# A two-phase FFN behind attention and a mixture of experts: buffers, conversions and token loads of its first phase rearranged

## Chip, cores and metric

One core of one Trainium2 chip. The time is device microseconds of a whole execution; that of a kernel is the median of its runs.

## What is computed

Linear attention over 4 x 8 heads, 576 positions and 64 features, then a routed mixture of 8 experts over the 2304 tokens, then a dense feed-forward network, all in float32 accuracy. The change lies in the last of the three:

```python
def _moe2_ref(x, w_in, w_out):            # x 2304 x 512, w_in 512 x 2048, w_out 2048 x 512
    h = x @ w_in
    g = np.maximum(0.01 * h, h)
    return (g @ w_out).astype(np.float32)

def reference(**kwargs):
    ...
    attn_out = _attn_ref(**attn_kwargs)
    ...
    x = _moe_ref(x=x, **moe_kwargs)
    return _moe2_ref(x=x, **moe2_kwargs)
```

The weights of the FFN arrive as float64, seen by the kernel as 64-bit integers.

## The kernel before

Every product is taken in three matmuls: both operands are split into a high and a low part (fp32r), and high x high, high x low and low x high are added in PSUM. `parts` (L1411, L1412) makes such a pair: ScalarE copies the value rounded to the high part, VectorE subtracts it to get the low part.

Attention and the experts come first (up to about 464 us of the profiled span); the experts leave their result, transposed, in DRAM as `yt`. The class `Ffn` does the rest. Its tokens are 9 groups j of 256, its hidden features 8 blocks b of 256. All work is in the order in which the program issues it: each engine takes its own instructions in that order, and waits in place where an operand or a buffer isn't ready. SP's queue, which issues the DMAs, is in order too.

**Phase one** makes h = leaky(x @ w_in). A step `first(b, j)` is 24 matmuls of 256 columns into one PSUM bank (four banks take turns). Then `leaky` (L1431, L1432): ScalarE writes 0.01 x bank into a tile `t`, VectorE takes the maximum of `t` and the bank, and `keep` (L1435) has SP store `t` in DRAM (`gd`, 256 KB). The bank is free after VectorE, the tile after the store has landed. The pool of `t` has 3 buffers. Block 0 and block 1 come interleaved, over all groups; blocks 2 to 7 follow, 9 steps each: 68 steps in `run`, the 4 other of the 72 products being made while the experts end (two by `wide`, whose halves `narrow` finishes at the start of `run`).

The tokens of the groups 4 to 8 are loaded in `run`: `load` (L1395) asks SP for 512 KB of `yt`, `x_split` makes the two parts.

The weights: `fetch` (L1345) asks SP for one block of float64, 1 MB, into the tile `wraw`. `cv1` (L1353 to L1356) takes the absolute value and the low words on ScalarE, sign and limits on VectorE; `cv2` joins exponent and mantissa on VectorE (L1361) and adds the rounding bits on GpSimd in two halves (L1363). Then for w_in (block numbers 0 to 7) `cv3` splits the result `af` into two parts; for w_out (8 to 15) `sums` (L1379 to L1381) makes 7 sums and differences of quarters of the block and `cv4` splits these. `wraw` has one buffer (tag raw) and `af` one. Weights 0 and 1 are converted long before; the other 14 here, two within each 9 steps. A table `work` in `run` says after which step each of these calls is issued.

**Phase two** makes h @ w_out in 7 products of halves instead of 8. `back` (L1455) loads two blocks of one group (512 KB) into one of three buffers of the pool f_raw, `combine` (L1462 to L1464) makes the sums on VectorE, `ready(k)` calls for a further combine where k is even, and splits one block's seven operands into the pair g[k] (five buffers in turn). `second(k)` is 21 matmuls (L1494). After 8 of them the group's result lies in four banks; `post` adds it up in four parts, multiplies by the token's gate, and `scatter` (L1534) has GpSimd write the rows by an indirect DMA. Four g are prepared ahead.

Of the kernel before, what the change touches and what calls it, by code (L numbers as in the profile page):

```python
# [8 lines left out]
F32 = mybir.dt.float32  # L9
# [4 lines left out]
I64 = mybir.dt.int64  # L14
AF = mybir.ActivationFunctionType
# [42 lines left out]
NB = 8  # L58
NG = 9
HELD = 4  # L60
PRODUCTS = ((1, 0), (5, 5), (0, 4), (4, 3), (2, 6), (6, 1), (3, 2))
CONVERT = 8

# [1224 lines left out]
class Ffn:  # L1288
# [23 lines left out]
    def open_x(self, ctx):  # L1312
        self.pad(ctx, "f_pad1", 48)
        self.slots.update(dict.fromkeys(("x0", "xh", "xl", "x3"), self.pool(ctx, "f_x0", 1)))
        self.t_p = self.pool(ctx, "f_t", 3)
        h, l = [self.slot(t, 2048, t).rearrange("p (j k n) -> p j k n", j=2, n=256) for t in ("xh", "xl")]
        self.wide_x = h, l
        for j in range(HELD):
            self.xs[j] = (h[:, j - 1], l[:, j - 1]) if j in (1, 2) else self.x_slot(j)
# [5 lines left out]
    def open_rest(self, ctx):  # L1325
        p = lambda n, b: self.pool(ctx, n, b, side="right")
        q = lambda n, b: self.pool(ctx, n, b, space=PSUM)
        self.pad(ctx, "f_pad2", eng=self.nc.gpsimd, side="right")
        self.slots.update(dict.fromkeys([f"{m}{b}" for m in "hl" for b in range(NB - 3)], p("f_v", 1)))
        self.slots.update(dict.fromkeys([f"x{j}" for j in range(HELD, NG)], p("f_x1", 1)))  # L1330
        self.raw_p, self.cv_p = p("f_raw", 3), p("f_cv", 1)
        self.early = False
        self.apart = p("f_apart", 1).tile([128, 8], F32, name="f_apart")
        ps_o = q("ps_o", 4)
        self.ps_o = lambda: ps_o.tile([128, DM], F32, tag="po", name="po")

        def ps_l():
            pool, tag = self.banks[self.turn % 4]
            self.turn += 1
            return pool.tile([128, 512], F32, tag=tag, name="pl")  # L1340
        self.turn, self.ps_l = 0, ps_l

    def fetch(self, i):
        t = self.cv_p.tile([128, 1024], I64, tag=("w0", "w2")[i] if self.early else "raw", name="wraw")
        self.nc.sync.dma_start(out=t, in_=self.wd[i])  # L1345
        half = lambda dt, j: t.bitcast(dt).rearrange("p (n t) -> p n t", t=2)[:, :, j]
        self.d[i] = {"hi": half(I32, 1), "hf": half(F32, 1), "lo": half(U32, 0), "li": half(I32, 0)}

    def cv1(self, i):
        nc, d = self.nc, self.d[i]  # L1350
        t = d["af"] = self.cv_p.tile([128, 2048], F32, tag=("w1", "w3")[i] if self.early else "af", name="af")
        d["f"], d["a"] = t[:, 0:1024].bitcast(I32), t[:, 1024:]
        nc.scalar.activation(d["a"], d["hf"], AF.Abs, scale=2.0 ** 16)  # L1353
        nc.scalar.activation(d["li"], d["lo"], AF.Copy, scale=2.0 ** -29)
        nc.vector.tensor_scalar(d["f"], d["hi"], -0x80000000, None, ALU.bitwise_and)
        nc.vector.tensor_scalar(d["a"], d["a"], F64_MAX, F64_MIN, ALU.min, ALU.max)  # L1356
# [94 lines left out]
    def back(self, p):  # L1451
        if p < NG * NB // 2:
            j, q = divmod(p, NB // 2)
            t = self.raws[p] = self.raw_p.tile([128, 1792], F32, tag="raw", name="raw").rearrange("p (b s n) -> p b s n", b=2, n=128)
            self.nc.sync.dma_start(out=t[:, :, 0:4], in_=self.gd[j][q].rearrange("p (b s n) -> p b s n", b=2, n=128))  # L1455

    def combine(self, p):
# [8 lines left out]
    def ready(self, k):  # L1466
        if k >= NG * NB:
            return
        p = k // 2
        if k % 2 == 0:  # L1470
            self.combine(p + 1)
        tag = ("wb", "x6", "x7", "wa", "x8")[k % 5]
        o = 0 if tag[0] == "w" else 16
# [24 lines left out]
    def post(self, j, part, last=False):  # L1498
# [11 lines left out]
        if part == 1:  # L1510
# [1 line left out]
            V.tensor_tensor(u[:, 1:3], u[:, 3:4].to_broadcast([128, 2, 256]), p1.rearrange("p (m n) -> p m n", n=256), ALU.add)  # L1512
            V.tensor_tensor(c0[:, h0], u[:, 1], p1[:, h1], ALU.add)
            if last:
                nc.scalar.activation(u[:, 0], u[:, 0], AF.Copy, scale=g1)
        elif part == 2:
            V.tensor_tensor(c0[:, h1], u[:, 1], p2[:, h0], ALU.add)
            nc.scalar.activation(c0, c0, AF.Copy, scale=g0)
            self.scatter(2 * j, c0)
            V.tensor_tensor(c1[:, h0], u[:, 2], p2[:, h1], ALU.add)  # L1520
            if last:
                nc.scalar.activation(c1[:, h0], c1[:, h0], AF.Copy, scale=g1)
        else:
            if last:
                V.scalar_tensor_tensor(c1[:, h1], p3[:, h0], g1, u[:, 0], ALU.mult, ALU.add)
            else:
                V.tensor_tensor(c1[:, h1], u[:, 0], p3[:, h0], ALU.add)
                nc.scalar.activation(c1, c1, AF.Copy, scale=g1)
            self.scatter(2 * j + 1, c1)
            del self.ms[j]  # L1530

# [9 lines left out]
    def run(self, ctx):  # L1541

        self.open_rest(ctx)
        self.load(HELD)
        self.load(HELD + 1)
        self.fetch(2)
        for j in range(HELD + 2, NG):
            self.load(j)
        self.narrow()
        steps = [(1, 1), (1, 2)] + [(b, j) for j in range(3, NG) for b in range(2)]  # L1550
        work = {5: [(self.cv1, 2)], 6: [(self.cv2, 2), (self.fetch, NB)], 7: [(self.cv3, 2)],
                10: [(self.cv1, NB)], 11: [(self.cv2, NB), (self.fetch, 3)], 12: [(self.sums, NB)], 13: [(self.cv4, NB)]}
        for s in (2, 4, 6, 8, 10):
            work.setdefault(s, []).insert(0, (self.x_split, HELD + s // 2 - 1))
        for b in range(2, NB):
            at = len(steps)
            steps += [(b, j) for j in range(NG)]
            i, o = b + 1, NB + b - 1
            if b < NB - 1:
                todo = {0: [(self.cv1, i)], 1: [(self.cv2, i), (self.fetch, o)], 2: [(self.cv3, i)], 4: [(self.cv1, o)],  # L1560
                        5: [(self.cv2, o), (self.fetch, i + 1 if b < NB - 2 else o + 1)], 6: [(self.sums, o)]}
                if b < NB - 2:
                    todo[7] = [(self.cv4, o)]
            else:
                todo = {0: [(self.back, 0), (self.back, 1)], 2: [(self.cv4, o - 1)], 3: [(self.cv1, o), (self.back, 2)],
                        4: [(self.cv2, o), (self.fetch, o + 1)], 5: [(self.sums, o), (self.cv4, o)],
                        6: [(self.combine, 0), (self.ready, 0)],
                        7: [(self.cv1, o + 1), (self.ready, 1)], 8: [(self.cv2, o + 1), (self.ready, 2), (self.ready, 3)]}
            for n, w in todo.items():
                work[at + n] = w  # L1570
        for s, (b, j) in enumerate(steps):
            self.first(b, j)
            for f, i in work.get(s, ()):
                f(i)
        end = NG * NB
        for k in range(end - 4):
            self.second(k)
            if k < 2:
                (self.sums, self.cv4)[k](2 * NB - 1)
# [233 lines left out]
```

## Time and profile before

| | us |
|---|---|
| Median of 3 runs (874.27 to 882.2) | 874.45 |
| The profiled execution | 873.44 |
| Its span in the profile | 871.2 |
| TensorE busy with matmuls (96% of the span) | 833.3 |
| VectorE busy (66%) | 574.1 |
| ScalarE busy (51%) | 440.5 |
| GpSimd busy (20%) | 172.6 |

The profile is one execution on the chip; times in it count from the start of its span. PE is TensorE (PEld its weight loads), DVE VectorE, ACT ScalarE, POOL GpSimd, SPq the queue of SP. In a row of a timeline stand start, duration, engine, line, operation, output and inputs, the number of like instructions merged into it, and in brackets the idle time of the engine ahead of it and what ended it. A merged row of several instructions of a queue spans from the first one's start to the last one's end. "pl" and "po" are PSUM banks, "t" the tile of an activation, "y" a loaded token group, "wraw" and "af" the two stages of a converted weight, "raw<-gd" a back.

### The profile page before, as it was taken

What the parts mean: (1) busy time and instruction counts of PE and PEld (TensorE: products, weight loads), DVE (VectorE), ACT (ScalarE), POOL (GpSimd) and SP (SyncE); (2) the same over time, 40 slices, a digit from 0 to 9 for tenths busy, and PEclk for the clock granted to TensorE, in tenths of its full rate; (3) what the DMA queues carried; (4) which work ended last, traced back from release to release, by engine and by line L of the source; (5) the groups of instructions that cost most, each with busy time, mean ns of one, the idle gap of its engine ahead of it and who ended that gap; (6) DMA issues with size and microseconds to landing.
All of it is one profiled execution on the core that took longest, in us unless ns stands there. A gap on an engine that the chain in (4) does not pass through costs nothing.

```text
span 871.2 us, 17587 instructions
## 1 busy us (share of the span) xinstructions
PE 833.3 (96%) x6850; PEld 819.3 (94%) x6850; DVE 574.1 (66%) x1065; ACT 440.5 (51%) x837; POOL 172.6 (20%) x236
## 2 busy tenths in 40 slices
PE   9999999999999999999998899999999599999996
PEld 8999999999999999999997789988999499999996
DVE  7678666876964275556771455555555898888883
ACT  7777666666343345466761444444343443445442
POOL 5345223322120110014300112121210201111112
PEclk9999999999999999999999899999999799999998
DMA  6452332162175234657747244535446334444431
GB/s 201 135 158 87 110 102 88 57 203 77 55 289 190 67 124 154 229 166 247 242 130 239 80 153 151 193 126 190 151 166 217 121 121 130 138 134 158 145 122 49
DMA packets 60809, 128.32 MB, mean 147 GB/s; under 512 B 5448, under 2 KB 24520, under 8 KB 58672
## 3 DMA queue, kind: packets, MB, share of 16 engines
q1 hardware_dynamic: 57520, 117.30, 41.0%
q0 software_dynamic: 3056, 9.70, 3.1%
q8 instruction: 56, 0.92, 0.4%
q14 instruction: 33, 0.27, 0.1%
q10 hardware_dynamic: 144, 0.13, 0.1%
HBM read 93.81 MB, written 33.29 MB: 146 GB/s over the span
## 4 chain that ended last, share of the span: by engine, by line
PE 68%; DVE 7%; DMA 7%; issue 5%; POOL 5%; ACT 5%; SPq 1%; POOLq 0%; ACTq 0%; DVEq 0%
PE po L1494 10%; PE pl L1494 9%; PE py L1208 8%; PE pp L1167 8%; PE kv L195 7%; PE nm L259 7%; PE pj L165 5%; DMA gd<-t 5%; POOL af L1363 4%; PE pl L1419 2%; DVE af L1361 2%; DMA wraw<-in_wd_dram 2%; PE dt L201 2%; PE py L1176 1%; PE ye L1027 1%
## 5 line engine op out<-in xcount | busy, mean ns | idle before, releaser
L1419 PE MATMUL pl<-x,wi 128*128 128x256 f32 x1296 | 157.6, 282 | 14.9 <-ACT x L1411 7.3
L1419 PEld LDWEIGHTS pl<-x,wi 128*128 128x128 f32 x1296 | 153.3, 192 | 18.9 <-DVE t L1432 8.1
L1494 PE MATMUL po<-wo,g 128*128 128x256 f32 x840 | 100.6, 282 | 10.6 <-ACT g L1411 8.0
L1494 PEld LDWEIGHTS po<-wo,g 128*128 128x128 f32 x840 | 99.1, 192 | 11.8 <-ACT g L1411 8.2
L1411 ACT ACTIVATE g<-raw 128x896 fp32r<-128x896 f32 x72 | 65.8, 946 | 42.4 <-DVE raw L1464 25.9
L1412 DVE TENSOR_TENSOR g<-raw,g 128x896 fp32r<-128x896 f32 x72 | 76.0, 1085 | 11.3 <-ACT g L1411 10.4
L1363 POOL TENSOR_TENSOR af<-af,wraw 128x512 int32<-128x512 int32 x32 | 41.5, 1319 | 194.6 <-DVE af L1361 194.6
L948 DVE TENSOR_TENSOR w<-raw,w 128x1024 fp32r<-128x1024 f32 x58 | 69.7, 1220 | 11.2 <-ACT w L941 10.7
L1494 PE MATMUL pl<-wo,g 128*128 128x256 f32 x672 | 76.8, 276 | 0.0
L1494 PEld LDWEIGHTS pl<-wo,g 128*128 128x128 f32 x672 | 76.5, 188 | 0.0
L1432 DVE TENSOR_TENSOR t<-t,pl 128x512 f32<-128x512 f32 x68 | 45.8, 683 | 46.3 <-ACT t L1431 46.2
L195 PE MATMUL kv<-v,kp 128*128 128x130 f32 x576 | 71.3, 276 | 0.4 <-ACT kvz L215 0.4
L1208 PE MATMUL py<-hp,w 128*128 128x344 f32 (+3 forms) x480 | 71.5, 305 | 0.0
L259 PE MATMUL nm<-kvz,qp 128*128 128x120 f32 (+2 forms) x576 | 69.8, 275 | 0.7 <-DVE xs L278 0.7
L259 PEld LDWEIGHTS nm<-kvz,qp 128*128 128x128 f32 x576 | 67.6, 191 | 1.0 <-PE ex L973 0.9
L1167 PE MATMUL pp<-p,w 128*128 128x344 f32 (+3 forms) x480 | 68.4, 302 | 0.0
L195 PEld LDWEIGHTS kv<-v,kp 128*128 128x128 f32 x576 | 67.5, 190 | 0.7 <-ACT kvz L215 0.6
L1208 PEld LDWEIGHTS py<-hp,w 128*128 128x128 f32 x480 | 67.5, 188 | 0.3
L1167 PEld LDWEIGHTS pp<-p,w 128*128 128x128 f32 x480 | 67.4, 188 | 0.0
L941 ACT ACTIVATE w<-raw 128x1024 fp32r<-128x1024 f32 x64 | 66.3, 1059 | 0.0
L1431 ACT ACTIVATE t<-pl 128x512 f32<-128x512 f32 x68 | 38.0, 592 | 55.1 <-DMA gd<-t 35.2
L959 POOL DMA_INDIRECT xg<-xd,idg x23 | 24.2, 1051 | 146.6 <-PE px L973 117.8
(356 smaller groups left out, 1545.5 us busy)
## 6 DMA issues: line engine op xcount, KB each, us to landing
raw<-in_wm_dram SPq DMA_DIRECT2D x64, 512.0 KB, 3.6
gd<-t SPq DMA_DIRECT2D x72, 256.0 KB, 4.0
raw<-gd SPq DMA_DIRECT2D x36, 512.0 KB, 3.9
wraw<-in_wd_dram SPq DMA_DIRECT2D x16, 1024.0 KB, 5.6
v<-in_v_dram SPq DMA_DIRECT2D x8, 650.0 KB, 6.3
raw<-in_kq_dram SPq DMA_DIRECT2D x7, 640.0 KB, 4.7
xd<-xs SPq DMA_DIRECT2D x32, 128.0 KB, 1.8
raw<-in_kq_dram SPq DMA_DIRECT2D x7, 512.0 KB, 4.0
```

The source lines that it names most:

```text
L195: nc.tensor.matmul(o, kp[:, f, 2 * i + h, :], r, start=(c == 0 and f == 0), stop=(c == 8 and f == 1), skip_group_check=True)
L259: nc.tensor.matmul(ov, qp[:, f, 2 * i + h, :], r, start=(f == 0), stop=(f == 1))
L941: nc.scalar.activation(hi, raw, AF.Copy)
L948: (eng or nc.vector).tensor_tensor(lo[:, h], raw[:, h], hi[:, h].bitcast(F32), ALU.subtract)
L1167: nc.tensor.matmul(pv[:, m], a[:, c], x[:, k], start=(k == 0 and i == 0), stop=(k == 3 and i == 2))
L1208: nc.tensor.matmul(p, a[:, c], b[:, k], start=(k == 0 and n == 0), stop=(k == 7 and n == 2))
L1363: nc.gpsimd.tensor_tensor(f[:, h], f[:, h], d["li"][:, h], ALU.add)
L1411: self.nc.scalar.activation(hi, t, AF.Copy)
L1412: self.nc.vector.tensor_tensor(lo, t, hi.bitcast(F32), ALU.subtract)
L1419: self.nc.tensor.matmul(o, a[:, c], x(k) if callable(x) else x[:, k], start=(k == 0 and n == 0), stop=(k == 3 and n == 2))
L1432: self.nc.vector.tensor_tensor(t, t, p, ALU.max)
L1494: self.nc.tensor.matmul(o, a[:, c], x[:, w], start=(b == 0 and n == 0 and m % 2 == 0), stop=(b == NB - 1 and n == 2 and m % 2 == 1 or b == ...
```

## The change

- The pool of `t` gets a fourth buffer.
- `wraw` and `af` get two homes each, four tags of one pool (raw, af, r0, r1) which a table `home` gives to the weights in turn; a fifth tag r2 joins r0 and r1 as the three buffers of `back`, in place of the pool f_raw.
- A table CONVERTED gives each weight its step t: `fetch` at t - 4, `cv1` at t, `cv2` at t + 1, `cv3` or `sums` at t + 3, `cv4` at t + 4, or, for the weights 13, 14 and 15, parked until step 61, 63 and 65. So a conversion begins about every fourth step, and the last (15) is done in phase one instead of in phase two.
- The loads of the groups 6, 7 and 8 are issued at the steps 2, 4 and 6, each as the split of the group two before is; `narrow` comes between the loads of 4 and 5.
- The backs 0 and 1 are asked for at step 61 (before: 59), the first combine follows at 62 (before: 65), and `ready` calls for the next combine at odd k instead of even.
- In the last `post` ScalarE multiplies what is known by the gates early, and one VectorE instruction each multiplies the last product by the gate and adds it.

Matmuls, their order and the DMAs' sizes and number stay.

```diff
+CONVERTED = ((2, 5), (8, 9), (3, 13), (9, 17), (4, 21), (10, 25), (11, 29), (5, 33), (12, 37), (6, 41), (13, 45), (7, 49), (14, 53),
+             (15, 57))
+PARKED = {13: 61, 14: 63, 15: 65}
...
-        self.t_p = self.pool(ctx, "f_t", 3)
+        self.t_p = self.pool(ctx, "f_t", 4)
...
-        self.raw_p, self.cv_p = p("f_raw", 3), p("f_cv", 1)
+        self.cv_p = p("f_cv", 1)
...
+        for c, (i, _) in enumerate(CONVERTED):
+            self.home[i] = ("raw", "r0")[c % 2], ("af", "r1")[c % 2]
+        self.home[14], self.home[15] = ("raw", "r1"), ("r0", "raw")
...
-            t = self.raws[p] = self.raw_p.tile([128, 1792], F32, tag="raw", name="raw").rearrange("p (b s n) -> p b s n", b=2, n=128)
+            t = self.raws[p] = self.cv_p.tile([128, 1792], F32, tag=("r2", "r0", "r1")[p % 3], name="raw").rearrange("p (b s n) -> p b s n", b=2, n=128)
...
-        if k % 2 == 0:
+        if k % 2:
             self.combine(p + 1)
...
             if last:
-                nc.scalar.activation(u[:, 0], u[:, 0], AF.Copy, scale=g1)
+                for o, i, g in ((c0[:, h1], u[:, 1], g0), (c0[:, h0], c0[:, h0], g0), (c1[:, h0], u[:, 2], g1), (c1[:, h1], u[:, 0], g1)):
+                    nc.scalar.activation(o, i, AF.Copy, scale=g)
+        elif last:
+            for c, h, p, g in ((c0, h1, p2[:, h0], g0), (c1, h0, p2[:, h1], g1)) if part == 2 else ((c1, h1, p3[:, h0], g1),):
+                V.scalar_tensor_tensor(c[:, h], p, g, c[:, h], ALU.mult, ALU.add)
+                if c is c0 or part == 3:
+                    self.scatter(2 * j + int(c is c1), c)
...
         self.load(HELD)
+        self.narrow()
         self.load(HELD + 1)
-        self.fetch(2)
-        for j in range(HELD + 2, NG):
-            self.load(j)
-        self.narrow()
...
+        for j in range(HELD, NG):
+            n = 2 * (j - HELD) + 2
+            work[n].append((self.x_split, j))
+            if j + 2 < NG:
+                work[n].append((self.load, j + 2))
+        for i, t in CONVERTED:
+            for n, f in ((t - 4, self.fetch), (t, self.cv1), (t + 1, self.cv2), (t + 3, self.cv3 if i < NB else self.sums)):
+                work[n].append((f, i))
+            if i >= NB:
+                work[PARKED.get(i, t + 4)].insert(0, (self.cv4, i))
+        for n, f, i in ((61, self.back, 0), (61, self.back, 1), (62, self.combine, 0), (64, self.back, 2), (64, self.ready, 0),
+                        (66, self.ready, 1), (67, self.ready, 2), (67, self.ready, 3)):
+            work[n].append((f, i))
```

**Order on SP, start of phase one.** Before, the first DMAs of `run`: `y<-yt` is a token load, `wraw` a weight fetch, `gd` a store of an activation.

```order
L1395 DMA y<-yt 128x4x256 x2
L1345 DMA wraw<-in_wd_dram 128x1024
L1395 DMA y<-yt 128x4x256 x3
L1435 DMA gd_0_78<-t 128x512
L1435 DMA gd_0_82<-t 128x512
L1435 DMA gd_0_78<-t 128x512
L1435 DMA gd_0_82<-t 128x512
```

The same place of the changed kernel, whose lines are seven further on:

```order
L1402 DMA y<-yt 128x4x256
L1442 DMA gd_0_78<-t 128x512
L1442 DMA gd_0_82<-t 128x512
L1402 DMA y<-yt 128x4x256
L1442 DMA gd_0_78<-t 128x512
L1442 DMA gd_0_82<-t 128x512
L1352 DMA wraw<-in_wd_dram 128x1024
L1442 DMA gd_0_86<-t 128x512
L1402 DMA y<-yt 128x4x256
L1442 DMA gd_0_86<-t 128x512
L1442 DMA gd_0_90<-t 128x512
L1402 DMA y<-yt 128x4x256
```

The stores now come ahead of the weight fetch, and the loads stand singly between them.

**Order on ScalarE, middle of phase one.** Before, a w_in weight and the w_out weight after it: `wi<-af` and `wo<-af` are splits, `af<-wraw` and `wraw<-wraw` are `cv1`, `t<-pl` the activation of one step each.

```order
L1411 ACTIVATE wi<-af 128x1024
L1431 ACTIVATE t<-pl 128x512 x2
L1353 ACTIVATE af<-wraw 128x1024
L1354 ACTIVATE wraw<-wraw 128x1024
L1431 ACTIVATE t<-pl 128x512 x3
L1411 ACTIVATE wo<-af 128x1792
L1431 ACTIVATE t<-pl 128x512 x2
L1353 ACTIVATE af<-wraw 128x1024
L1354 ACTIVATE wraw<-wraw 128x1024
```

The changed kernel, the like place:

```order
L1418 ACTIVATE wi<-af 128x1024
L1438 ACTIVATE t<-pl 128x512
L1360 ACTIVATE af<-wraw 128x1024
L1361 ACTIVATE wraw<-wraw 128x1024
L1438 ACTIVATE t<-pl 128x512 x4
L1418 ACTIVATE wo<-af 128x1792
L1360 ACTIVATE af<-wraw 128x1024
L1361 ACTIVATE wraw<-wraw 128x1024
L1438 ACTIVATE t<-pl 128x512 x3
L1418 ACTIVATE wi<-af 128x1024
```

A split now stands three or four activations behind the `cv1` of its weight; before, two or three. The `cv1` of the next weight follows at once or after one activation.

**Order on VectorE, end of phase one.** Before, from the last split of w_out there to the last step: `raw<-raw` are the three instructions of a combine, `g<-raw,g` the low part of a g, `t<-t,pl` the maximum of one step each.

```order
L1412 TENSOR_TENSOR wo<-af,wo 128x1792
L1432 TENSOR_TENSOR t<-t,pl 128x512
L1462 TENSOR_TENSOR raw<-raw 128x2x128
L1463 TENSOR_TENSOR raw<-raw 128x2x2x128
L1464 TENSOR_TENSOR raw<-raw 128x2x128
L1462 TENSOR_TENSOR raw<-raw 128x2x128
L1463 TENSOR_TENSOR raw<-raw 128x2x2x128
L1464 TENSOR_TENSOR raw<-raw 128x2x128
L1412 TENSOR_TENSOR g<-raw,g 128x896
L1432 TENSOR_TENSOR t<-t,pl 128x512
L1355 TENSOR_SCALAR af<-wraw 128x1024
L1356 TENSOR_SCALAR af<-af 128x1024
```

The changed kernel, from the split of weight 14 to the second g:

```order
L1419 TENSOR_TENSOR wo<-af,wo 128x1792
L1439 TENSOR_TENSOR t<-t,pl 128x512
L1419 TENSOR_TENSOR g<-raw,g 128x896
L1439 TENSOR_TENSOR t<-t,pl 128x512
L1419 TENSOR_TENSOR wo<-af,wo 128x1792
L1439 TENSOR_TENSOR t<-t,pl 128x512
L1469 TENSOR_TENSOR raw<-raw 128x2x128
L1470 TENSOR_TENSOR raw<-raw 128x2x2x128
L1471 TENSOR_TENSOR raw<-raw 128x2x128
L1419 TENSOR_TENSOR g<-raw,g 128x896
L1439 TENSOR_TENSOR t<-t,pl 128x512
```

The first g comes three steps earlier, a single combine stands ahead of the second g, and the last weight's `cv1` is no longer there.

## Rows read from the trace of the kernel before

**Rows 1.** Busy time of each engine by stretch, then granted clock, DMA share, GB/s.

```profile
464.00:677.68 213.68, 196.89 (x1632) 191.88 (x1632) 109.32 (x143) 84.14 (x111) 33.55 (x27) 0.98 0.49 166
685.69:864.60 178.91, 176.11 (x1512) 174.93 (x1512) 155.03 (x239) 83.14 (x104) 20.62 (x35) 0.98 0.38 124
715.00:845.00 130.00, 130.00 (x1149) 130.00 (x1149) 115.01 (x182) 60.17 (x75) 15.39 (x28) 1.00 0.43 140
```

**Rows 2.** Timeline of TensorE: first and last matmuls of phase one, first of two.

```profile
464.13 0.36 PE L1419 MATMUL pl<-xh,wi 128*128 128x256 f32 x1
...
670.80 6.88 PE L1419 MATMUL pl<-x,wi 128*128 128x256 f32 x57
685.69 0.80 PE L1494 MATMUL po<-wo,g 128*128 128x256 f32 x2 [8.01 <-ACT g L1411]
```

**Rows 3.** Timeline of the tail: the last sum and the last scatter.

```profile
864.55 0.48 DVE L1525 SCALAR_TENSOR_TENSOR c<-po,gate,u 128x256 f32<-128x256 f32 x1 [0.69 <-PE po L1494]
...
865.85 0.98 POOL L1534 DMA_INDIRECT out_dram<-c,idc  x1 [0.19 <-issue]
```

**Rows 4.** The chain that ended last, one piece of phase two.

```profile
711.80 19.04 PE pl L1494 x168
```

**Rows 5.** TensorE alone by stretch: busy (matmuls), granted clock, DMA share, GB/s.

```profile
464.13:490.00 25.87, 18.70 (x137) 0.87 0.62 204
510.00:677.68 167.68, 160.34 (x1363) 1.00 0.48 164
```

**Rows 6.** Timeline of SP and ScalarE, start of phase one.

```profile
466.76 4.03 SPq L1395 DMA_DIRECT2D y<-yt  x3
...
470.85 24.94 SPq L1435 DMA_DIRECT2D gd<-t  x9
479.93 1.24 ACT L1431 ACTIVATE t<-pl 128x512 f32<-128x512 f32 x2 [12.09 <-DMA gd<-t]
```

**Rows 7.** Timeline of SP and ScalarE, one conversion in the middle of phase one.

```profile
558.92 0.33 SPq L1345 DMA_DIRECT2D wraw<-in_wd_dram  x1
558.93 1.06 ACT L1411 ACTIVATE wi<-af 128x1024 fp32r<-128x1024 f32 x1 [4.22 <-POOL af L1363]
```

**Rows 8.** Waits from 464 to 691: us in total, times, longest.

```profile
ACT t L1431 <- DMA gd<-t: 35.2, 8, 12.1
...
PE pl L1419 <- DVE t L1432: 6.8, 13, 0.9
```

**Rows 9.** Timeline of VectorE between the phases.

```profile
680.51 2.02 DVE L1412 TENSOR_TENSOR wo<-af,wo 128x1792 fp32r<-128x1792 f32 x1 [1.82 <-ACT wo L1411]
...
682.45 0.68 DVE L1432 TENSOR_TENSOR t<-t,pl 128x512 f32<-128x512 f32 x1
...
683.50 0.69 DVE L1463 TENSOR_TENSOR raw<-raw 128x512 f32<-128x512 f32 x1
...
684.23 0.42 DVE L1464 TENSOR_TENSOR raw<-raw 128x256 f32<-128x256 f32 x1
...
686.09 1.08 DVE L1412 TENSOR_TENSOR g<-raw,g 128x896 fp32r<-128x896 f32 x1
```

**Rows 10.** Timeline of ScalarE and VectorE at a token split.

```profile
494.12 0.60 ACT L1431 ACTIVATE t<-pl 128x512 f32<-128x512 f32 x1 [0.35 <-PE pl L1419]
494.62 1.05 ACT L1411 ACTIVATE x<-y 128x1024 fp32r<-128x1024 f32 x1
495.70 1.23 DVE L1412 TENSOR_TENSOR x<-y,x 128x1024 fp32r<-128x1024 f32 x1 [0.26 <-ACT x L1411]
```

**Rows 11.** DMA: a store's time to landing; backs between 465 and 690 (KB, median us).

```profile
DMA to landing us min/median/max: 2.0/4.0/7.5
...
raw<-gd SPq DMA_DIRECT2D x3, 512.0 KB, 5.7
```

**Rows 12.** Timeline of VectorE, a combine while GpSimd adds (692.13 to 695.14).

```profile
692.27 1.72 DVE L1463 TENSOR_TENSOR raw<-raw 128x512 f32<-128x512 f32 x1
694.02 1.41 DVE L1464 TENSOR_TENSOR raw<-raw 128x256 f32<-128x256 f32 x1
```

**Rows 13.** Busy time by stretch, as rows 1, behind short waits at a token split.

```profile
503.00:508.00 5.00, 3.39 (x15) 3.20 (x16) 2.53 (x4) 0.86 (x2) 0.00 (x0) 0.68 0.88 338
```

More of the change, by code (lines that the diff above doesn't have):

```diff
@@ L1330, in open_rest @@
         self.slots.update(dict.fromkeys([f"x{j}" for j in range(HELD, NG)], p("f_x1", 1)))
-        self.raw_p, self.cv_p = p("f_raw", 3), p("f_cv", 1)
+        self.cv_p = p("f_cv", 1)
         self.early = False
+        self.home = {}
+        for c, (i, _) in enumerate(CONVERTED):
+            self.home[i] = ("raw", "r0")[c % 2], ("af", "r1")[c % 2]
+        self.home[14], self.home[15] = ("raw", "r1"), ("r0", "raw")
         self.apart = p("f_apart", 1).tile([128, 8], F32, name="f_apart")
@@ L1343, in fetch @@
     def fetch(self, i):
-        t = self.cv_p.tile([128, 1024], I64, tag=("w0", "w2")[i] if self.early else "raw", name="wraw")
+        t = self.cv_p.tile([128, 1024], I64, tag=("w0", "w2")[i] if self.early else self.home[i][0], name="wraw")
         self.nc.sync.dma_start(out=t, in_=self.wd[i])
@@ L1350, in cv1 @@
         nc, d = self.nc, self.d[i]
-        t = d["af"] = self.cv_p.tile([128, 2048], F32, tag=("w1", "w3")[i] if self.early else "af", name="af")
+        t = d["af"] = self.cv_p.tile([128, 2048], F32, tag=("w1", "w3")[i] if self.early else self.home[i][1], name="af")
         d["f"], d["a"] = t[:, 0:1024].bitcast(I32), t[:, 1024:]
@@ L1520, in post @@
             V.tensor_tensor(c1[:, h0], u[:, 2], p2[:, h1], ALU.add)
-            if last:
-                nc.scalar.activation(c1[:, h0], c1[:, h0], AF.Copy, scale=g1)
-        else:
[L1524 to L1528, printed above, removed]
+        else:
+            V.tensor_tensor(c1[:, h1], u[:, 0], p3[:, h0], ALU.add)
+            nc.scalar.activation(c1, c1, AF.Copy, scale=g1)
             self.scatter(2 * j + 1, c1)
@@ L1544, in run @@
         self.load(HELD)
+        self.narrow()
         self.load(HELD + 1)
-        self.fetch(2)
-        for j in range(HELD + 2, NG):
-            self.load(j)
-        self.narrow()
[L1550 to L1570, printed above, removed]
+        steps = [(1, 1), (1, 2)] + [(b, j) for j in range(3, NG) for b in range(2)] + [(b, j) for b in range(2, NB) for j in range(NG)]
@@ new lines, in run @@
+        work = {n: [] for n in range(len(steps))}
+        for j in range(HELD, NG):
[8 more added lines that the diff above has]
+                work[PARKED.get(i, t + 4)].insert(0, (self.cv4, i))
@@ L1571, in run @@
+        for n, f, i in ((61, self.back, 0), (61, self.back, 1), (62, self.combine, 0), (64, self.back, 2), (64, self.ready, 0),
+                        (66, self.ready, 1), (67, self.ready, 2), (67, self.ready, 3)):
+            work[n].append((f, i))
         for s, (b, j) in enumerate(steps):
             self.first(b, j)
-            for f, i in work.get(s, ()):
+            for f, i in work[s]:
                 f(i)
@@ L1577, in run @@
             self.second(k)
-            if k < 2:
-                (self.sums, self.cv4)[k](2 * NB - 1)
             self.ready(k + 4)
```

## The prediction

> **What bounds the kernel now.** I read, in this order: busy time by stretch; the timeline of TensorE at the borders of the two FFN phases; the chain that ended last; the waits in phase one; and the timelines of SP, ScalarE and VectorE where TensorE had stood still. TensorE is the bound, so everything is counted in matmuls that it did not start.
>
> Phase one is 68 steps of 24 matmuls, 1632 in all, from the first one at 464.13 to 670.80 + 6.88 = 677.68 [rows 1, 2]: 213.55 us. Phase two is 9 x 8 x 21 = 1512 matmuls from 685.69 to 864.5, where the last VectorE instruction had stopped waiting for TensorE [rows 1, 2, 3]: 178.8 us. What a matmul takes where nothing is late shows in the chain: 168 of them in 19.04 us, 0.1133 us each, so 2.72 us a step [rows 4]. At that pace phase one is 1632 x 0.1133 = 185.0 us and phase two 171.4 us. So 28.6 us are lost in phase one, 8.0 us between the phases (the gap is written at the row of 685.69), and 7.4 us in phase two: 44.0 us is all there is to win in the code that the change touches.
>
> Where the 28.6 us lie: the first 25.87 us hold 137 matmuls, worth 15.5 us, so 10.3 are lost there. The last 167.68 us hold 1363, worth 154.5, so 13.2 are lost there. Some 5 us are left for the 20 us between [rows 5].
>
> The reasons are not the same. **At the start**, SP puts a weight fetch of 1 MB and three token loads of 0.5 MB ahead of all stores; the loads alone keep SP to 470.79, the first store leaves at 470.85, and ScalarE stands still for 12.09 us until a store has landed and a t buffer is free [rows 6]. With t not free no PSUM bank is emptied. **Later** the cycle is that of one raw and one af buffer: the fetch waits on SP until GpSimd's second add is done (558.92), and ScalarE, already at the split that is issued one step after the adds, waits 4.22 us for them (558.93) [rows 7]; activations of two steps queue behind that split, their stores leave late, and t is short again. In sum ScalarE waited 35.2 us for stores, 8 times, and TensorE 6.8 us in 13 waits of at most 0.9 us for the bank that VectorE frees [rows 8]. **Between the phases** VectorE has a conversion of w_out, both first combines and the first g in a row ahead of TensorE [rows 9], and in phase two's first 20 us still a last conversion.
>
> **The change part by part.** It removes no matmul and no byte. VectorE was busy 109.3 us and ScalarE 84.1 us in phase one [rows 1]: 59% and 45% of 185.0 us. About 8 us of VectorE work (the last conversion, one combine) move in. Neither can be the bound there on average; only order and buffers can cost.
>
> *Loads one by one, the fetch after them.* A load now has four steps, 10.9 us, until its split, and waits only behind one or two stores. The 10.3 us go. What is late next: each x_split is issued two steps before its use. In the trace the activation after the step's end starts at 494.12 and the split's low part ends at 495.70 + 1.23 = 496.93, 2.8 us after the step's end, against 2.72 us for one step [rows 10]: 0.2 us of wait for each of the five splits. Before two of them ScalarE has a conversion in the step ahead (0.25 us more each): 1.5 us. Bounds: 0, if the first matmuls, which need only the high part, cover it; 5 x 1.05, one whole copy each, above.
>
> *Two raw and two af buffers, a conversion every fourth step.* The split or the sums follow the adds by two steps instead of one, and a fetch is asked for three steps after the adds that free its buffer, so SP no longer waits for GpSimd. I take these waits as gone, and with them 13.2 us and most of the 5 between.
>
> *Four t buffers.* A store has four steps, 10.9 us, less about 1.3 for activation and maximum, to land. Landings took 2.0 to 7.5 us, median 4.0 [rows 11]. This holds even behind a 1 MB fetch. I take 0; the bounds are under the rivals.
>
> *The border.* GpSimd's adds are over by then, but three splits of w_out (2.02 us each on VectorE) are parked in the last seven steps. From the end of step 61 VectorE must do, up to the low part of the second g: seven maxima at 0.68, three splits at 2.02, two combines at 0.42 + 0.69 + 0.42, two g at 1.08, together 16.0 us [rows 9], and TensorE wants that g at 6 x 2.72 + 2.38 = 18.7 us. It fits, unless the first back, asked for one step before its combine, is late: VectorE comes to the combine at 5.2 us; the request leaves at about 1.6 and took 5.7 us to land in this stretch [rows 11], so VectorE stands some 2 us and the rest ends near 19.6. TensorE waits 0.9 us; from 0 (landing in 4.0 us, the stores' median) to 3. The 8.0 us are gone. In phase two the last conversion is gone, so the loss of 7.4 us goes with it; VectorE was busy 115.0 of 130 us there and TensorE never stood [rows 1].
>
> *combine one call later.* Its three instructions stay; its input has one call more to land, and its result one less ahead of its use. Four prepared g lie between, so 0.
>
> *The tail.* The last scatter left at 865.85, behind the one before it. Now the product by the gate is fused for both halves: the first leaves earlier, the second after 864.55 + 0.48 = 865.03 [rows 3]. That is 0.75 us, at most 1, at least 0.
>
> At one place a rule speaks against the change. At 692.27, beside GpSimd's adds, a combine's instructions took 1.72 and 1.41 us instead of 0.69 and 0.42 [rows 9, 12]. The Trainium skill says so too (SBUF — State Buffer, Who interferes with whom): a VectorE instruction with two SBUF inputs and a GpSimd one that reads SBUF exclude each other for a whole instruction; here the trace agrees. By that rule the adds, now beside the fourth token split, would hold it for about 1 us, once, and the sum would be 833.1 instead of 832.1.
>
> **The sum**, on the profiled execution: 464.13 + 185.0 + 1.5 (splits) = 650.6 for the end of phase one, + 171.4 + 0.9 = 822.9 against 864.5. That is 41.6 less, and 0.75 from the tail: 42.3. The execution took 873.44 us, of which the span was 871.2, so 831.1. The median of the three runs is 1.0 above this execution: **832.1**.
>
> **The rivals.**
> - *Stores still land late.* 14 fetches of 1 MB still cross with 68 stores. For it: 35.2 us of waits end with a landing [rows 8]. Against: those stores left late, they did not travel long. If half of what lies behind the first stall stays, (13.2 + 5) / 2 = 9 us: 841.
> - *The border is a new wait.* VectorE is close to full over seven steps. If the back lands late and the adds of the fifteenth conversion reach into it, half of what border and start of phase two cost now, (8.0 + 7.4) / 2 = 7.7, stays instead of 0.9: 839.
> - *The clock.* Behind short waits for a token split the granted clock in 503 to 508 was 0.68, that is 3.2 us at the lower of its levels (1.2 and 2.4 GHz), which costs 1.6 us [rows 13]. The Trainium skill warns of that (TensorE: Matmul & The Clock Gate, A second HAM failure mode: psum-queue depth-cycling): short idle times between groups of matmuls can make the clock go down and up. If each of the five splits did that, 5 x 1.6 = 8 us: 840. Against: 13 waits of up to 0.9 us from 510 on left the clock at 1.00 [rows 5, 8].
> - *Slower: phase two becomes VectorE's.* A pair of g costs VectorE 155.0 / 36 = 4.3 us with all that goes with it [rows 1]; TensorE takes 4.76. Were each combine, one call later and so nearer to the scatters, to take what it took beside GpSimd, 0.42 + 1.72 + 1.41 instead of 1.53 [rows 12], the pair would be 6.3 us, and 36 pairs cost 36 x 1.55 = 56 us: 888. It decides from 4.76 + 42 / 36 = 5.9 us a pair. Against: GpSimd then has only 18 scatters, and 130 us with scatters in them ran dense [rows 1].
> - *It does not do what it says*: the same waits under other buffers. 870.
>
> **How the numbers follow.** Forecast as summed 0.68, late stores 0.13, border 0.09, clock 0.05, slower 0.03, no effect 0.02. With no wait at all the sum is 829.7; runs differ by 0.3%, so the low end is 827. The first four cases reach 841; with two of them at once, or one dearer than I put it, 846. Within 1% is about what a measurement of this kernel can tell from no change. Faster by more: 0.95; same 0.02; slower 0.03.
>
> **What would show it.** Right: phase one near 187 us from first to last matmul, no ScalarE wait of over 3 us for a store, SP never waiting for GpSimd, under 1.5 us between the phases, the clock at 1.00 from 464 on. Wrong: waits for t or for a store in the steady steps; a gap of several us before phase two with VectorE busy; a clock under 1.00; phase two over 174 us.

## The result, and the profile after

The changed kernel takes **830.6 us** (median of 4 runs, 830.3 to 831.0), the kernel before 874.4 us (4 runs): a ratio of 0.949, 95% interval 0.944 to 0.954. Forecast were 832.1 us, in a range from 827 to 846. The profiled execution took 830.34 us, its span 828.6. One run of all below, of experiment 6, was slow (842.85 us, over 1.5% above the fastest of its kernel) and is left out.

Busy time of each engine, the stretches that answer to [rows 1]: phase one, phase two and 130 us out of phase two; then granted clock, DMA share, GB/s.

```profile
463.63:650.50 186.87, 186.62 (x1633) 185.68 (x1634) 122.20 (x161) 94.38 (x119) 36.08 (x28) 1.00 0.58 198
650.62:822.00 171.38, 171.35 (x1512) 171.16 (x1511) 146.37 (x229) 80.07 (x100) 19.19 (x33) 1.00 0.39 130
672.00:802.00 130.00, 130.00 (x1150) 130.00 (x1149) 113.95 (x180) 61.76 (x76) 16.99 (x28) 1.00 0.42 140
```

Phase one went from 213.6 to 186.9 us with the same matmuls, the gap of 8.0 us is gone, phase two went from 178.8 to 171.4 us: 42.1 us in all, of the 42.6 by which the span is shorter. The other 0.5 us lie ahead of phase one, which begins at 463.63 instead of 464.13; the variants of both kernels begin it anywhere from 463.57 to 464.25. The granted clock is 1.00 in all three stretches.

The chain that ended last, start, length and what. In [rows 4] one piece of phase two stood for seven; here the chain is TensorE alone from the fourth token split on.

```profile
474.93 2.89 PE pl L1426 x23
...
478.34 1.06 ACT x L1418
...
479.42 1.24 DVE x L1419
...
480.70 2.89 PE pl L1426 x23
...
492.25 158.36 PE pl L1426 x1391
650.62 19.04 PE po L1501 x168
669.65 19.04 PE pl L1501 x168
```

The first pieces repeat every 5.77 us, which is two steps (5.44) and 0.3 us more: TensorE waits for the low part of each token split, as [rows 10] let one expect. From 492.25 on the chain never leaves it: 1391 matmuls in 158.36 us are 0.1138 us each. The fifth split still holds up one weight load, for 0.16 us at 498.12.

The waits from 464 to 660, against [rows 8]:

```profile
ACT t L1438 <- PE pl L1426: 86.6, 52, 2.5
...
ACT wi L1418 <- POOL af L1370: 5.5, 4, 1.6
...
DVE raw L1469 <- DMA raw<-gd: 0.9, 1, 0.9
```

ScalarE now waits for TensorE (86.6 us), no longer for stores (35.2 us before), and a little for GpSimd's adds: 5.5 us in all where it was 24.5, and 1.6 at most where it was 4.22 [rows 7].

### The profile page after: what moved, and what is told of

Same layout as the page of the kernel before. It is cut to its first block, busy times and chain, and to the rows that moved or that the text cites. A ratio compares the mean times of both kernels' runs of the same rounds, so it can differ in the third digit from the quotient of the medians.

```text
span 828.6 us, 17583 instructions
## 1 busy us (share of the span) xinstructions
PE 817.9 (99%) x6850; PEld 809.0 (98%) x6850; DVE 572.5 (69%) x1065; ACT 444.5 (54%) x838; POOL 173.6 (21%) x236
## 3 DMA queue, kind: packets, MB, share of 16 engines
q1 hardware_dynamic: 57520, 117.30, 42.6%
## 5 line engine op out<-in xcount | busy, mean ns | idle before, releaser
L1426 PE MATMUL pl<-x,wi 128*128 128x256 f32 x1296 | 149.5, 277 | 0.3
L1426 PEld LDWEIGHTS pl<-x,wi 128*128 128x128 f32 x1296 | 148.0, 188 | 1.2 <-DVE x L1419 1.2
L1501 PE MATMUL po<-wo,g 128*128 128x256 f32 x840 | 96.0, 276 | 0.0
L1501 PEld LDWEIGHTS po<-wo,g 128*128 128x128 f32 x840 | 95.6, 188 | 0.0
L1419 DVE TENSOR_TENSOR g<-raw,g 128x896 fp32r<-128x896 f32 x72 | 78.3, 1087 | 16.0 <-ACT g L1418 16.0
L1438 ACT ACTIVATE t<-pl 128x512 f32<-128x512 f32 x68 | 40.6, 597 | 86.7 <-PE pl L1426 86.6
L1542 POOL DMA_INDIRECT out_dram<-c,idc x18 | 19.2, 1068 | 171.5 <-ACT c L1531 150.1
```

Of the source, the lines that this page charges most:

```text
L1419: self.nc.vector.tensor_tensor(lo, t, hi.bitcast(F32), ALU.subtract)
L1426: self.nc.tensor.matmul(o, a[:, c], x(k) if callable(x) else x[:, k], start=(k == 0 and n == 0), stop=(k == 3 and n == 2))
L1501: self.nc.tensor.matmul(o, a[:, c], x[:, w], start=(b == 0 and n == 0 and m % 2 == 0), stop=(b == NB - 1 and n == 2 and m % 2 == 1 or b == ...
```

## Experiments

Twelve variants were timed, each beside the kernel before on one chip; the ratios are to the runs of the kernel before there, whose medians were 873.1 to 878.2 us. The first seven are edits of the changed kernel (830.6 us), and the fourth goes on from the third; the last five are edits of the kernel before.

### 1. The start put back, in the changed kernel

```diff
         self.load(HELD)
-        self.narrow()
         self.load(HELD + 1)
+        self.fetch(2)
+        for j in range(HELD + 2, NG):
+            self.load(j)
+        self.narrow()
```

and the later calls of these loads and this fetch left out.

> The changed kernel, but with its token loads and the first weight fetch asked for at once again, ahead of all stores, as in the kernel before (830.6 us is the changed kernel). Theory A (the first stall is the order on SP: stores leave late, the activation that waits for one holds up the token split behind it on ScalarE, and TensorE needs that split, however many t buffers there are): 8 to 11 us come back, 839 to 842, with a TensorE gap of 6 to 7 us near 475. Theory B (the fourth t buffer and the four banks cover it): 831 to 834.

Measured 840.6 us (839.6 to 840.8), ratio to before 0.961 (0.957 to 0.966). Timeline of SP, ScalarE and TensorE at the start:

```profile
470.77 12.70 SPq L1442 DMA_DIRECT2D gd<-t  x6
479.73 0.60 ACT L1438 ACTIVATE t<-pl 128x512 f32<-128x512 f32 x1 [9.32 <-DMA gd<-t]
480.22 1.05 ACT L1418 ACTIVATE x<-y 128x1024 fp32r<-128x1024 f32 x1
...
481.32 0.58 PE L1426 MATMUL pl<-x,wi 128*128 128x256 f32 x1 [6.11 <-ACT x L1418]
```

The stores leave at 470.77, behind the loads, as in [rows 6]. With four t buffers ScalarE comes one step further, but the activation that waits (9.32 us) stands ahead of the token split, and TensorE waits for the split, 6.11 us. Theory A: order on SP, not the number of buffers. The whole 10 us that the start cost come back. In the kernel before TensorE stood for the same split, as its waits from 464 to 691 show; the first 25.87 us hold 137 matmuls in both.

```profile
PE pl L1419 <- ACT x L1411: 7.3, 2, 6.5
```

### 2. Three t buffers, in the changed kernel

```diff
-        self.t_p = self.pool(ctx, "f_t", 4)
+        self.t_p = self.pool(ctx, "f_t", 3)
```

> The changed kernel with three t buffers again. Theory A (stores that leave in time land within three steps, less the 1.3 us of activation and maximum: 6.8 us against a median of 2.5 us after the change): 830.5 to 832. Theory B (the fourth buffer is what pays): 838 or more, with ScalarE waits for stores.

Measured 831.1 us (830.7 to 831.4), ratio 0.951 (0.946 to 0.955): 0.5 us, which is within the noise. TensorE waits nowhere in phase one that it does not wait in the changed kernel. Theory A.

### 3. One raw buffer, in the changed kernel

```diff
-            self.home[i] = ("raw", "r0")[c % 2], ("af", "r1")[c % 2]
+            self.home[i] = "raw", ("af", "r1")[c % 2]
...
-            for n, f in ((t - 4, self.fetch), (t, self.cv1), ...
+            for n, f in ((t - 3, self.fetch), (t, self.cv1), ...
```

> The changed kernel with one raw buffer for all weights but the last; each fetch is issued one step later, behind the adds that free the buffer, so SP waits for GpSimd again. Theory A (what hurt TensorE was ScalarE standing before the split; SP's wait of about 1 us a fetch only delays stores that have slack): ScalarE waits some 2 us for each fetch at cv1, TensorE under 2 us in all: 830.5 to 833. Theory B (the second raw buffer is what pays in the steady part): half or more of 18 us comes back, 839 or more.

Measured 864.7 us (861.8 to 866.7), ratio 0.989 (0.984 to 0.994). **34 us come back**: theory A fell, and more comes back than the 18 us of which B speaks. One turn of the conversion in the timeline of all engines but TensorE:

```profile
574.19 0.33 SPq L1352 DMA_DIRECT2D wraw<-in_wd_dram  x1
...
580.73 1.15 ACT L1360 ACTIVATE af<-wraw 128x1024 f32<-128x1024 f32 x1 [3.13 <-DMA wraw<-in_wd_dram]
...
584.02 1.22 DVE L1368 SCALAR_TENSOR_TENSOR af<-af 128x1024 int32<-128x1024 int32 x1
...
585.47 2.57 POOL L1370 TENSOR_TENSOR af<-af,wraw 128x512 int32<-128x512 int32 x2 [11.31 <-DVE af L1368]
588.07 0.33 SPq L1352 DMA_DIRECT2D wraw<-in_wd_dram  x1
```

These are not separate waits but a ring: the fetch (6.5 us until `cv1` starts), `cv1`, the activations that had queued behind it on ScalarE, the joining on VectorE, the adds, and only then the next fetch, since the adds read the low words out of the raw buffer. A turn takes 13.6 us as a mean over eight (520.39 to 629.04). The program gives it four steps, 10.9 us. As each step's activation stands in program order behind its `cv1`, TensorE can get ahead of the ring by no more than the banks and then goes at the ring's pace: 13 turns x 2.7 us = 35 us at most. TensorE's own waits (four groups: for t, g and twice x) add up to 24.2 us in this execution; beside them stand matmuls that went slower, as 341 in 40.00 us from 510 to 550 (0.1173 us each) at a granted clock of 1.00, and stretches in which that clock was lower: 0.93 in the mean from 464 to 510, 0.96 from 650 to 690. The ring explains the waits; how much of the remaining 10 us follows from them was not tried apart. The ring is the new theory, called L from here, and what the next experiments were to test.

### 4. The same, with a shorter ring

```diff
-            for n, f in ((t - 3, self.fetch), (t, self.cv1), (t + 1, self.cv2), ...
+            for n, f in ((t - 4, self.fetch), (t, self.cv1), (t, self.cv2), ...
```

> The kernel with one raw buffer again (864.7 us), its conversion loop shortened: the joining on VectorE and GpSimd's adds are issued in the step of cv1, ahead of the waiting activations, and the next fetch right behind them. Theory L (one raw buffer makes a closed loop, fetch, landing, cv1, joining, adds, next fetch, of 13.7 us a conversion against 10.9 us for the four steps it stands beside, and TensorE follows the loop): the loop becomes about 12.3 us, some 1.4 us less for each of 13 conversions: 843 to 850. Theory S (the cost is that stores stand behind a fetch that waits on SP): as before, 860 or more.

Measured 852.6 us (845.4 to 853.0), ratio 0.972 (0.967 to 0.978). Its fetches, the first and the last of eight in the timeline of SP:

```profile
540.03 0.33 SPq L1352 DMA_DIRECT2D wraw<-in_wd_dram  x1
...
627.35 0.33 SPq L1352 DMA_DIRECT2D wraw<-in_wd_dram  x1
```

A turn now takes 12.5 us (87.32 / 7), 1.1 less, as L expected (12.3). The gain is 12 us in the median, and the median is above L's range of 843 to 850; the fastest run lies inside. In the profiled execution all of phase two went at 19.79 us for 168 matmuls instead of 19.04 (last section), which is 6.8 us over its 1512. Phase one alone is what the ring should shorten: from its first matmul to the first of phase two it took 202.3 us (463.61 to 665.88), in experiment 3 215.8 (463.98 to 679.82). That is 13.5 us, against 13 turns x 1.1 = 14.3; the two executions also differ in clock and pace, so the agreement is a rough one. Theory S, 860 or more, fell.

### 5. Splits one step after the adds, in the changed kernel

```diff
-..., (t + 3, self.cv3 if i < NB else self.sums)):
+..., (t + 2, self.cv3 if i < NB else self.sums)):
```

> The changed kernel with split and sums one step after the adds instead of two, so that ScalarE stands in front of GpSimd's adds again, as in the kernel before. Theory L (only a loop longer than its steps costs TensorE; a wait of ScalarE alone is taken up by four banks and four t buffers): ScalarE waits some 2 us or more for each of 5 weights of w_in, TensorE none: 830.3 to 831.5. Theory A (that wait is what made stores late): 836 or more.

Measured 833.0 us (832.7 to 833.4), ratio 0.953 (0.948 to 0.957): 2.3 us more, between both. ScalarE waits 21.8 us in 6 waits for the adds again (5.5 us in the changed kernel), up to 4.3 us. All of TensorE's waits in phase one, by its timeline:

```profile
493.21 0.38 PE L1426 MATMUL pl<-x,wi 128*128 128x256 f32 x1 [0.85 <-ACT x L1418]
494.77 14.11 PE L1426 MATMUL pl<-x,wi 128*128 128x256 f32 x119 [1.18 <-DVE x L1419]
```

It is one place, where a token split stands behind the waiting split of the first weight. The five like waits later cost nothing: from 510 to 650 TensorE was busy for all 140.00 us, with 1238 matmuls. So L holds in the steady steps, and a wait of ScalarE costs where something without a reserve stands behind it.

### 6. Token splits one step earlier, in the changed kernel

```diff
-            n = 2 * (j - HELD) + 2
+            n = 2 * (j - HELD) + 1
```

> The changed kernel with each token split and the load that goes with it one step earlier, three steps before its use. If the five waits of TensorE for a split's low part (0.2 to 0.3 us each in the trace) are what phase one still has over 185.0 us: 829.0 to 829.8. If the loads, asked for four steps ahead as before but against a split that is earlier too, or the first split, come late: 831 or more.

Measured **829.0 us** (median of 5, fastest 828.7), ratio 0.948 (0.944 to 0.952): 1.6 us less than the changed kernel, the best of all that was run. The two ratios' intervals overlap; what shows the gain is the chain:

```profile
464.20 185.22 PE pl L1426 x1632
649.43 19.04 PE po L1501 x168
```

All 1632 matmuls of phase one are one piece of 185.2 us instead of 186.9, at the pace of [rows 4]. Nothing is left to win in the order of this phase.

### 7. Both combines ahead of the first g, in the changed kernel

```diff
-        for n, f, i in (..., (62, self.combine, 0), (64, self.back, 2), (64, self.ready, 0),
+        for n, f, i in (..., (65, self.combine, 0), (64, self.back, 2), (65, self.ready, 0),
...
-        if k % 2:
+        if k % 2 == 0:
             self.combine(p + 1)
```

> The changed kernel with the first two combines and the first g issued together at step 65 again, and further combines called at even k; conversions stay as changed. Theory A (at the border VectorE's order decides): both combines stand ahead of the first g on VectorE, TensorE waits 2 to 4 us between the phases: 833 to 835. Theory B (the gap came from the conversions alone, those of weights 14 and 15): no gap, 830.5 to 831.

Measured 836.0 us (833.7 to 841.7), ratio 0.956 (0.951 to 0.960). Timeline of TensorE at the border, in the slowest of the six executions (841.7 us), which is the one that was profiled:

```profile
652.19 0.50 PE L1501 MATMUL po<-wo,g 128*128 128x256 f32 x2 [1.40 <-ACT g L1418]
653.74 2.47 PE L1501 MATMUL po<-wo,g 128*128 128x256 f32 x13 [1.04 <-DVE g L1419]
```

TensorE waits 2.4 us, inside A's 2 to 4, but the median lies above A's range; only the fastest run (833.7) is inside. Behind these waits the granted clock was 0.80 from 656 to 661, and phase two went at the slower pace of the last section, which makes up 6.8 of the 11 us in this execution. VectorE's order at the border costs by itself. Most of the kernel before's 8.0 us is something else, though: there work of the last two weights came on top, which was not tried alone.

### 8. The new start alone, in the kernel before

```diff
         self.load(HELD)
-        self.load(HELD + 1)
-        self.fetch(2)
-        for j in range(HELD + 2, NG):
-            self.load(j)
         self.narrow()
+        self.load(HELD + 1)
...
+            work[s].insert(1, (self.load, HELD + s // 2 + 1))
+        work[1] = [(self.fetch, 2)]
```

The loads come singly and the fetch behind the first two steps, as in the change; the rest is as before.

> The kernel before (874.4 us) with nothing but the changed order at the start: loads singly, narrow's stores and the first two steps' stores ahead of the weight fetch. Theory A (order on SP made the first stall): the 10.3 us of the first 26 us go and most of what followed until 510, 860 to 865. Theory B (three t buffers would stall there anyway): under 4 us, 870 or more.

Measured 863.1 us (861.2 to 870.1), ratio 0.990 (0.984 to 0.996): 10 us less in the median, 9 by the ratio. In its first 25.87 us stand 218 matmuls where [rows 5] have 137. Theory A; about the same 10 us as in experiment 1, seen from the other side.

### 9. The fourth t buffer alone, in the kernel before

```diff
-        self.t_p = self.pool(ctx, "f_t", 3)
+        self.t_p = self.pool(ctx, "f_t", 4)
```

> The kernel before with a fourth t buffer and nothing else. Theory A (late stores are the cause, the buffer only a margin; the steady waits for t, some 0.5 us of TensorE each, can shrink): the first stall stays, 866 to 872. Theory B (the buffer is what pays): the steady part's 13 us and some of the first stall go, 855 to 861.

Measured 866.3 us, ratio 0.993 (0.991 to 0.996): 7 us less in the median, 6 by the ratio, inside A's range. So the buffer is worth some 7 us in the kernel before and nothing clear of noise in the changed one (experiment 2). Its fetches come every 13.3 us (514.80 to 647.48, ten turns) against 13.7 before (518.20 to 654.79, ten turns): by L it pays as ScalarE gets sooner to the next `cv1`, which is argued and was not tried apart.

### 10. Splits two steps after the adds, in the kernel before

```diff
-..., 2: [(self.cv3, i)], ... 6: [(self.sums, o)]}
+..., 3: [(self.cv3, i)], ... 7: [(self.sums, o)]}
...
-                    todo[7] = [(self.cv4, o)]
+                    todo[8] = [(self.cv4, o)]
```

> The kernel before with the weights' split, sums and the split after the sums issued one step later (two steps after the adds instead of one), one raw and one af buffer as before. Theory A (ScalarE standing before the split for GpSimd is what makes stores late in the steady part): 8 to 13 us go, 861 to 867. Theory B (the single raw buffer, with SP waiting for GpSimd ahead of the stores, is the cause): under 4 us, 870 or more.

Measured 877.4 us, ratio 1.004 (1.001 to 1.007): **not faster but 4 us slower**, as theory B allows. ScalarE's waits, from 464 to 690:

```profile
ACT t L1431 <- DMA gd<-t: 52.9, 14, 12.7
...
ACT af L1353 <- DMA wraw<-in_wd_dram: 26.6, 6, 5.1
...
ACT wi L1411 <- POOL af L1363: 14.6, 5, 3.7
```

ScalarE waits less for the adds, 14.6 us where it was 24.5, and more for stores, 52.9 us where it was 35.2. A turn of the ring takes 14.2 us (517.32 to 659.44, ten turns). The split, one step later, now stands one activation ahead of the next `cv1` instead of two, and `cv1` is in the ring; that this lengthens the turn is argued from the order. So two steps instead of one do not cure the late stores. As the wait for the adds was not taken away, only shortened, this experiment alone does not clear it; experiments 5 and 12 do.

### 11. Fetches from GpSimd's queue, in the kernel before

```diff
-        self.nc.sync.dma_start(out=t, in_=self.wd[i])
+        (self.nc.sync if self.early else self.nc.gpsimd).dma_start(out=t, in_=self.wd[i])
```

> The kernel before with the weight fetches asked for by GpSimd's own queue instead of SP's, so that no store stands behind a fetch that waits for the adds; one raw and one af buffer as before. Theory A (ScalarE's wait before the split is the cause): the steady part gains little, and the first stall stays since the loads still stand ahead of the stores: 870 to 875. Theory B (SP's wait ahead of the stores is the cause): 8 to 13 us go, 861 to 867.

Measured 865.1 us, ratio 0.992 (0.989 to 0.995): 8 us, the low end of theory B. No store stands behind a fetch any more, and a turn takes 13.1 us (514.97 to 606.76, seven turns). That is 0.55 us less than before, and some 7 us over 13 turns, so the experiment does not tell stores that leave sooner from a shorter ring. The ring stays longer than its steps, and the waits at the start and at the border stay too (5.1 and 5.6 us of TensorE).

### 12. A second raw buffer alone, in the kernel before

```diff
-        self.raw_p, self.cv_p = p("f_raw", 3), p("f_cv", 1)
+        self.cv_p = p("f_cv", 1)
...
-... tag=("w0", "w2")[i] if self.early else "raw", name="wraw")
+... tag=("w0", "w2")[i] if self.early else "r0" if 8 <= i <= 13 else "raw", name="wraw")
...
-            t = self.raws[p] = self.raw_p.tile([128, 1792], F32, tag="raw", ...
+            t = self.raws[p] = self.cv_p.tile([128, 1792], F32, tag=("r2", "r0", "r1")[p % 3], ...
```

> The kernel before (873 to 874 us) with a second raw buffer and nothing else: weights of w_in and 14 and 15 in one, 8 to 13 of w_out in the other, which a back uses later; every call stays where it was, one af buffer, three t. Theory L (the closed loop through one raw buffer, two turns of some 13.7 us against 24.5 us for nine steps, is what TensorE follows in the steady part): fetches no longer wait for GpSimd, the two turns stand in 24.5 us, 13 to 17 us go, 857 to 861; the first stall and the gap between the phases stay. Other theory (single af, three t buffers or ScalarE's wait for the adds hold the pace as well): under 6 us, 868 or more.

The second buffer, r0, is one that a back uses later. Measured 856.2 us (854.1 to 857.3), ratio 0.974 (0.971 to 0.977): by the ratio 23 us less than the runs of before beside it (878.2 in this comparison), 18 us less than the 874.4 of the others; L had expected 13 to 17. Between the two profiled executions it is 16.6 us. TensorE alone, by stretch, as [rows 5], what is left of its waits in phase one, and a wait of ScalarE from 464 to 690:

```profile
464.13:490.00 25.87, 18.82 (x142) 0.80 0.60 207
490.00:510.00 20.00, 17.91 (x137) 0.91 0.36 128
510.00:664.00 154.00, 153.94 (x1357) 1.00 0.54 185
```

```profile
481.29 0.58 PE L1419 MATMUL pl<-x,wi 128*128 128x256 f32 x1 [6.37 <-ACT x L1411]
...
502.72 0.38 PE L1419 MATMUL pl<-x,wi 128*128 128x256 f32 x1 [0.85 <-ACT x L1411]
```

```profile
ACT wi L1411 <- POOL af L1363: 16.5, 6, 4.2
```

From 510 on TensorE is full, 1357 matmuls in 154 us, with three t buffers, one af buffer and the split at its old place; the stalls at the start and at 503 stay. ScalarE still waits for the adds, six times and up to 4.2 us, and TensorE loses nothing by it in the steady steps. The gap before phase two went from 8.0 to 4.0 us, which L had not expected. The second raw buffer is the one part that the steady steps needed.

## Why the prediction was right

The sum stood at 831.1 us for the profiled execution and came out at 830.34. Part of that closeness is luck: border and tail were off by 0.8 and 0.6 us in opposite directions, and 0.5 us came from the earlier start of phase one, which no part of the sum contains. By its steps:

- **The method held.** 1632 and 1512 matmuls at the undisturbed pace, plus named waits: phase one 185.0 + 1.5 forecast, 186.9 measured; phase two 171.4 and 171.4.
- **The start:** 10.3 us forecast; put back it costs 10.0, alone it brings about 10. The order on SP was the cause, as described. What TensorE stood for was not quite what the prediction says (no bank emptied): it was the token split, queued on ScalarE behind the waiting activation, 6.5 us in the kernel before and 6.1 with the start put back.
- **The token splits:** forecast at 0.2 us for each of five and 0.5 for two conversions ahead, 1.5 us. Phase one came out 1.9 us over its 185.0; taken away (experiment 6) the waits gave 1.7. The slowing of a split beside GpSimd's adds, priced at 1 us, did not come: the adds ran from 487.78 to 490.35, the fourth split's low part began at 490.97 and took 1.23 us, as in [rows 10].
- **The steady part:** the 13.2 us and most of the 5 between went, as forecast, and the second raw buffer alone takes the 13.2. **The step that failed is the reason given for it**: that ScalarE's wait of 4.22 us for the adds holds up the activations and so the stores, and that two steps instead of one would cure it. With two raw buffers ScalarE may wait up to 4.3 us for the adds and it costs nothing in the steady steps (experiments 5 and 12); with one, the later split made the kernel slower (experiment 10). What holds is the ring through the one raw buffer, 13.7 us a turn where nine steps for two turns allow 12.2. The prediction named the single buffer and the fetch behind the adds, but added them up as two waits instead of closing the ring and comparing its length with its steps. The change cures both, so the sum was not touched: that the number was right in spite of the wrong reason is luck. Nor were the 13.2 us all waits: by [rows 5], as the profile counts it, TensorE was idle for 7.3 of the 167.68 us and busy for 160.34 with 1363 matmuls, 0.1176 us each, where the prediction counts 0.1133 (last section).
- **Four t buffers:** 0 forecast, 0.5 us measured in the changed kernel, within the noise. In the kernel before the same buffer is worth some 7 us: here the reserve paid only as long as something was late.
- **The border:** 0.9 us forecast, 0.1 measured. The 16.0 us of work and 2 of standing that the prediction lists make 18.0; for the 1.6 us up to its 19.6 it gives no row. VectorE did wait for the first back, 0.92 us instead of 2, and the second g was ready in time, as its timeline shows:

```profile
640.09 0.43 DVE L1469 TENSOR_TENSOR raw<-raw 128x256 f32<-128x256 f32 x1 [0.92 <-DMA raw<-gd]
...
644.75 1.08 DVE L1419 TENSOR_TENSOR g<-raw,g 128x896 fp32r<-128x896 f32 x1
...
651.50 1.08 DVE L1419 TENSOR_TENSOR g<-raw,g 128x896 fp32r<-128x896 f32 x1
```

  It ends at 652.6, and TensorE's first 21 matmuls of phase two run until about 653.0.
- **The tail:** 0.75 us forecast, about 0.1 measured; compare [rows 3]:

```profile
820.73 0.87 DVE L1526 SCALAR_TENSOR_TENSOR c<-po,gate,c 128x256 f32<-128x256 f32 x2 [1.66 <-PE po L1501]
821.98 0.98 POOL L1542 DMA_INDIRECT out_dram<-c,idc  x1 [6.33 <-issue]
822.08 0.48 DVE L1526 SCALAR_TENSOR_TENSOR c<-po,gate,c 128x256 f32<-128x256 f32 x1 [0.48 <-PE po L1501]
...
823.26 0.98 POOL L1542 DMA_INDIRECT out_dram<-c,idc  x1 [0.18 <-issue]
```

  The last scatter starts 1.18 us after VectorE's last instruction begins; it was 1.30. The forecast let it start when that instruction ends, but it stands behind the scatter before it on GpSimd, which leaves at 821.98, some 0.8 us after its own data (the first half of the pair at 820.73). What holds that one was not tried.

The rivals: late stores did not stay; ScalarE waited for none of them. The clock did not fall, although the five short waits came: the granted clock was 1.00. The Trainium skill warns (TensorE: Matmul & The Clock Gate, A second HAM failure mode: psum-queue depth-cycling) that short idle times between groups of matmuls can make the clock go down and up. The trace after does not show that: four waits of 0.26 us for a weight load, 5.8 us apart, and a fifth of 0.16 left it at 1.00. VectorE did not become the bound of phase two: 114.0 of 130 us busy, 115.0 before.

Put side by side, the parts alone in the kernel before bring 10 (start), 17 to 23 (raw buffer, of which 4 at the border) and some 7 us (t buffer; by L another way into the same loss). The rest of the 44 us is the border and the last conversion, of which experiment 7 shows 2.4 us of wait to be the order of the combines (3.1 us by its fastest run, 5.4 by its median); the share of the last conversion alone was not tried.

## What to carry to other kernels

Where a buffer is filled, worked on by several engines and filled again, follow the ring from one fill to the next and compare its length with the work that it stands beside: with a ring of 13.6 us beside 10.9 us of matmuls the kernel took 34 us more, though none of TensorE's own waits on it was over 2.8 us. Here a second buffer for the one tile that closed the ring opened it; a reserve elsewhere paid only while something was late. On a queue in order, ask of each long request what short ones stand behind it, and who holds a buffer for them.

## What was not expected of the hardware

TensorE has two paces at the same granted clock of 1.00. In the experiment with both combines ahead of the first g, one piece of the chain in phase two is

```profile
694.87 19.79 PE po L1501 x168
```

against 19.04 us for the same 168 matmuls in the changed kernel: 0.1178 us each instead of 0.1133, 4% more. There phase one had gone at 0.1136 (1295 matmuls in 147.05 us), and the slower pace began behind the waits at the border and lasted to the end. The profiled execution of experiment 4 shows it too. Over both phases, 3144 matmuls, this is 14 us. What sets the pace stays open; in this execution a gap of 2.4 us was followed by a loss longer than itself.

Nor did like waits always bring the granted clock down. Behind 0.85 and 1.18 us at one token split it was 0.79 and 0.64 in the kernel before (503 to 506, 506 to 509) and 0.70 and 0.73 in experiment 12 (the same stretches), but 1.00 in experiment 5 (494 to 500), behind waits of the same length. What makes the difference stays open.
